# Working out the RMS norm's factor on a PSUM tile, with Newton's products in another order

## The chip, the core and the metric

The kernel runs on one core of a Trainium2 chip. The metric is the device time of one execution in microseconds (us). Before the change three executions took 826.66, 829.93 and 831.51 us: the median is 829.93 us.

## What is computed

Three blocks follow one another (cut from the reference):

```python
# 1 clustered attention, 2 batches x 8 heads, 768 tokens, head size 64
mask = q_assign[:, :, :, None] == k_assign[:, :, None, :]
scores = np.where(mask, scale * q @ k.T, -1e9); attn = softmax(scores); x = attn @ v
# 2 gated block on (1536, 512): RMS norm, two products to 1536, one back to 512
rms = np.sqrt(np.mean(x * x, axis=-1, keepdims=True) + 1e-06)
xn = x / rms * rms_g
g = xn @ w_gate
x = (g / (1 + np.exp(-g)) * (xn @ w_val)) @ w_out
# 3 second block: h = x @ w_in, s * relu(h)**2 + b, @ w_out2
```

The change lies in the line that computes `rms`: the kernel needs 1/rms for every token.

## The kernel before

**Stages.** Attention works head by head (16 heads, 8 of each batch). For each head the scores of 128 keys by 768 queries are made on PE (`scores`, L447 and L448), exponentiated on ACT (`expo`, L453), split into an fp16 high part (`cast`, on ACT at L460 or on POOL at L458) and an fp16 rest (`rest`, POOL, L464, tile `al`), and multiplied with the values on PE (`pv_chunk`, L487 and L477). Ahead of that, per head, PE makes row maxima of the scores (`rowmax`, L416, tile `mps`), which DVE reduces (`rowmax_out`, L424, tile `mt`). DVE also copies the head's result out (`pv_out`, L498 to L500, tile `xt`).

**The norm.** When a batch's 8 heads are done, `rms_sq` and `rms_sq2` (L516 to L524) square and sum them into `ss`, six columns for the six chunks of 128 tokens. `rms_scale` (from L528) adds the two halves of `ss` (L530), scales them (L531) and calls `rsqrt` (L504 on), which makes a first guess with integer operations on the bits (L506, L507) and refines it with three Newton steps of three instructions each (L509, L510, L511). That is 13 DVE instructions on tiles of 128x6 elements, and before the change every operand lies in SBUF. For each chunk, `rms_norm` (L539) then multiplies the row by the factor and by `g_row` into `xn`, PE transposes it (`rms_tr`, L546, tile `tr`), ACT makes the high part (`rms_x`, L553, `xh`) and DVE the low part (L555, `xl`).

**What follows.** The first gated-block products of batch 0 are mixed into the attention of batch 1 (`m_mm`, `m_pr`); the rest of both blocks comes after the attention, where PE works on long runs of matmuls (L623, L656, L658).

**What sets the order.** A planner (`Plan`) takes every step with an engine, a cost, its dependencies and a due time worked out from the table `P`, and writes one fixed instruction order for each engine. Buffers of a tag (`s` has 3 PSUM tiles, `g` has 2) are handed out in that order. Each engine then runs its own list in order and waits on semaphores. The pool of the tag `g` (`ps_g0`) takes over the PSUM of the second row-maximum tile when the plan's step `switch` runs.

The same `rsqrt` also serves `centroid_scale` at the very start of the kernel, on tiles of 128x1 that stay in SBUF.

Of the kernel before, what the change touches and what calls it, by code (L numbers as in the profile page):

```python
# [20 lines left out]
F32 = mybir.dt.float32  # L21
# [6 lines left out]
ALU = mybir.AluOpType  # L28
# [16 lines left out]
class Plan:  # L45
# [8 lines left out]
    def add(self, eng, dur, fn, r=(), w=(), new=(), prio=0.0, lat=None):  # L54
        deps = set()
        n = len(self.ops)
        for key in r:
            if key in self.last_w:
                deps.add(self.last_w[key])
        for key in w:  # L60
            deps.update(self.readers.get(key, ()))
            if key in self.last_w:
                deps.add(self.last_w[key])
        for key in r:
            self.readers.setdefault(key, []).append(n)
        for key in w:
            self.last_w[key] = n
            self.readers[key] = []
        for t in {key[:2] for key in (*r, *w)}:
            self.users.setdefault(t, []).append(n)  # L70
        self.ops.append((eng, dur, fn, deps, new, prio, lat))
# [74 lines left out]
def attention_moe_moe2_kernel(  # L146
# [18 lines left out]
    B, H, S, D = q.shape  # L165
# [5 lines left out]
    NCH = S // 128  # L171
# [8 lines left out]
    PSUM = bass.MemoryType.PSUM  # L180
    dma = nc.sync.dma_start
    act = nc.scalar.activation
    tt = nc.vector.tensor_tensor
    stt = nc.vector.scalar_tensor_tensor

    def pool(stack, name, bufs=1, **kw):
        return stack.enter_context(tc.tile_pool(name=name, bufs=bufs, **kw))
# [9 lines left out]
    ps_g = []  # L197
# [21 lines left out]
    sm = pool(att, "sm")  # L219
# [7 lines left out]
    ps_s = pool(att_a, "ps_s", P["b_s"], space=PSUM)  # L227
    ps_v = pool(att_a, "ps_v", P["b_pv"], space=PSUM)
    att_m = ExitStack()
# [8 lines left out]
    ss = [big.tile([128, NCH, 2], F32, name=f"ss{i}") for i in range(B)]  # L238
# [265 lines left out]
    def rsqrt(y, x, w):  # L504

        nc.vector.tensor_scalar(w.bitcast(I32), x.bitcast(I32), 1, None, op0=ALU.logical_shift_right)  # L506
        nc.vector.tensor_scalar(y.bitcast(I32), w.bitcast(I32), -1.0, float(0x5F3759DF), op0=ALU.mult, op1=ALU.add)  # L507
        for _ in range(3):
            tt(out=w, in0=y, in1=y, op=ALU.mult)  # L509
            stt(out=w, in0=w, scalar=-0.5, in1=x, op0=ALU.mult, op1=ALU.mult)  # L510
            stt(out=y, in0=w, scalar=1.5, in1=y, op0=ALU.add, op1=ALU.mult)  # L511

    def rms_sq(b, c, h0, h1, j):
# [12 lines left out]
    jk2 = {}  # L526

    def rms_scale(b):  # L528
        x, r, w = (sm.tile([128, NCH], F32, tag=f"{n}{b}", name=n) for n in ("rx", "rr", "rw"))
        tt(out=x, in0=ss[b][:, :, 0], in1=ss[b][:, :, 1], op=ALU.add)  # L530
        nc.vector.tensor_scalar(x, x, 1.0 / DM, 1e-6, op0=ALU.mult, op1=ALU.add)  # L531
        rsqrt(r, x, w)
        r_t[b] = r
        for t in range(b * S // TB, (b + 1) * S // TB):
            xh[t], xl[t] = new_x(t)
# [210 lines left out]
    add = pl.add  # L746
# [6 lines left out]
    def call(fn, *args):  # L753
        return lambda: fn(*args)
# [40 lines left out]
    def last_head():  # L795
        early.close()
        xpool[2] = xpool[3] = pool(ctx, "x1p", side="right")

    for i in range(NH):
        b, h = heads(i)  # L800
        p = i // 2

        def at(lead, more=0):
            return NCH * i - P[lead][b] - more + (P["ho"][i] if i < len(P["ho"]) else 0)

        if i % 2 == 0:
            if i:
                add("SP", 2.2, call(load, i), r=[("q4", 0, "m") if i == 2 else ("lseq", i - 2)], w=[("t", i), ("t", i + 1), ("lseq", i)], new=[("t", i), ("t", i + 1)],
                    prio=at("lq"), lat=5.2)
            add("SP", .48, call(load_v, i), r=[("q4", 0, "m")] if i == 2 else [], w=[("vr", i), ("vr", i + 1)], new=[("vr", i), ("vr", i + 1)],  # L810
                prio=at("lw"), lat=1.7)
            add("ACT", 1.03, call(v_square, i), r=[("vr", i), ("vr", i + 1)], w=[("v2", p)], new=[("v2", p)],
                prio=at("ly"))
# [26 lines left out]
        for c in range(NCH):  # L840
            add("PE", .36, call(rowmax, i, c), r=[("q4", i, x) for x in ("qh", "b1", "m")], w=[(mk(i, c), (i, c))], new=[(mk(i, c), (i, c))],
                prio=at("lm", -c))
            add("DVE", .95, call(rowmax_out, i, c), r=[(mk(i, c), (i, c)), *([("maxed", i, 0)] if c else [])], w=[("mt", i), ("maxed", i, c)], new=[("mt", i)] if c == 0 else (),
                prio=at("lm", -c))
# [4 lines left out]
        if P["nat"][i]:  # L849
            add("ACT", .19 + .05 * P["nat"][i], call(prep_v3, i), r=[("vr", i), ("vsc", p), ("vs", i, "h")], w=[("vs", i, "n"), ("loaded_v", i, "n")],  # L850
                prio=at("lv"))
        add("POOL", .08, call(prep_one, i), r=[("vs", i, "h"), ("vs", i, "n")], w=[("vs", i, "1")], prio=at("lv"))
        add("DVE", .2 * (NCH - P["nat"][i]), call(prep_v2, i), r=[("vr", i), ("vsc", p), ("vs", i, "h")], w=[("vs", i, "l"), ("loaded_v", i)], prio=at("lv"))
        for c in range(NCH):
            for e in range(2):
                add("PE", .36, call(scores, i, c, e), r=[("q4", i, x) for x in ("qh", "m", "x", "b1", "b2", "ql", "kl", "lt")],
                    w=[("s", (i, c, e)), ("scored", i, c, e)], new=[("s", (i, c, e))], prio=at("ls", -c))
                add("ACT", .49, call(expo, i, c, e), r=[("s", (i, c, e))], w=[("a", (i, c))],
                    new=[("a", (i, c))] if e == 0 else (), prio=at("ls", -c))
            if c >= NCH - P["nat"][i]:  # L860
# [3 lines left out]
                prio=at("lc", -c))  # L864
        for c0 in range(0, NCH, P["pvb"]):
# [5 lines left out]
                w=[("pv", i)], new=[("pv", i)] if c0 == 0 else (), prio=at("lp", -c0))  # L871
        add("DVE", 1.0, call(pv_out, i), r=[("pv", i), ("vsc", p)], w=[("xt", b, h)], new=[("xt", b)] if h == 0 else (),
            prio=at("lz"))
# [8 lines left out]
        if i == NH - 1:  # L882
            add("SP", 0.0, last_head, r=[(x, n) for x in ("loaded_u", "loaded_v") for n in range(NH)] + [("loaded_v", n, "n") for n in range(NH)] + [("scored", n, c, e) for n in range(NH) for c in range(NCH) for e in range(2)], w=[("r", 1)], prio=-1e5)
        if h == H - 1:
            add("DVE", 2.4, call(rms_scale, b), r=[("ss", b, c, x) for c in range(NCH) for x in (H - 3, H - 1)],
                w=[("r", b)], prio=at("lr"))
            for c in range(NCH):
                g = ("s", ("r", b, c))
                add("DVE", .89, call(rms_norm, b, c), r=[("r", b), ("g_row", 0), *(("xt", b, x) for x in range(H))],
                    w=[("xn", (b, c))], new=[("xn", (b, c))], prio=at("lr"))  # L890
                add("PE", .43, call(rms_tr, b, c), r=[("xn", (b, c))], w=[g], new=[g], prio=at("lr"))
                t = b * (S // TB) + c * 128 // TB
                add("ACT", .6, call(rms_x, b, c, 0), r=[g], w=[("x", t, "h", c)], prio=at("lr"))
                add("DVE", .68, call(rms_x, b, c, 1), r=[g, ("x", t, "h", c)], w=[("x", t, "l", c)], prio=at("lr"))
# [55 lines left out]
    def m_acc(n, t, c):  # L950
        project_add(pg_t.pop((n, t, "p", c)), t, c, TB, n == 0)

    def switch():
        att_m.close()
        ps_g.append(pool(att_m, "ps_g0", P["b_g"], space=PSUM))

    def m_xh(t, c):
        if c == 0:
            xh[t], xl[t] = new_x(t)
# [2 lines left out]
    def m_xl(t, c):  # L962
        nc.gpsimd.tensor_tensor(
            out=xl[t][:, c], in0=acc[t][:, c * TB:c * TB + TB], in1=xh[t][:, c].bitcast(F32), op=ALU.subtract
        )

    add("SP", 0.0, switch, r=[("maxed", H - 1, c) for c in range(NCH)], w=[("gsw", 0)], prio=-1e5)

    def gx(t, part):
        return [("x", t, part, c) for c in range(t * TB // 128, (t + 1) * TB // 128)]  # L970
# [80 lines left out]
```

## Time and profile before

| | us |
|---|---|
| median of three executions | 829.93 |
| lowest, highest | 826.66, 831.51 |
| the profiled execution, its own time | 827.66 |
| its span, first to last instruction | 825.7 |
| PE busy in the span | 780.9 |
| DVE busy | 519.4 |
| ACT busy | 469.1 |
| POOL busy | 444.4 |

The span is what the trace covers; 2.0 us lie around it. PE is TensorE's matmul, PEld its weight load, DVE VectorE, ACT ScalarE, POOL GpSimd, SP the queue that issues the DMAs. A duration in the trace runs from the start of an instruction to its end, so an instruction that is held up after its start shows a long duration and no idle time before it. In the table of stages, PEclk is the granted share of TensorE's full clock of 2.4 GHz; 0.50 is 1.2 GHz.

### The profile page before, as it was taken

How to read it: one execution, taken by the hardware profiler on the slowest of the kernel's cores; microseconds unless marked ns; L12 is line 12 of the kernel's file. 1: busy time of each engine (PE TensorE's matmuls, PEld its weight loads, DVE VectorE, ACT ScalarE, POOL GpSimd, SP SyncE). 2: the span in 40 equal slices, each digit the busy share in tenths (PEclk: the TensorE clock that was granted, in tenths of full speed). 3: DMA queues.
4: the chain of work that ended last, by engine and by line, in shares of the span. 5: the costliest groups of instructions: out<-in, count | busy, mean ns of one | idle time of the engine just before them, and what ended most of it. 6: DMA issues, size and time to landing. Idle time of an engine off the chain costs nothing.

```text
span 825.7 us, 14199 instructions
## 1 busy us (share of the span) xinstructions
PE 780.9 (95%) x5505; PEld 722.5 (88%) x5505; DVE 519.4 (63%) x845; ACT 469.1 (57%) x883; POOL 444.4 (54%) x400
## 2 busy tenths in 40 slices
PE   3899898699999799999999999999999999999998
PEld 1688776589998689999999999998999998989897
DVE  6789898898876676554645446554465555555533
ACT  5486778556858555442434435555566566665532
POOL 7599999677999534332323226455343343343421
PEclk9999999799999999999999999999999999999999
DMA  7498766155430223311311212220121121220012
GB/s 114 86 138 146 159 135 122 30 106 134 98 87 27 78 77 102 101 55 50 102 51 56 72 52 78 82 93 30 32 97 52 52 77 52 78 74 29 1 39 114
DMA packets 98818, 65.13 MB, mean 79 GB/s; under 512 B 64992, under 2 KB 89664, under 8 KB 98752
## 3 DMA queue, kind: packets, MB, share of 16 engines
q1 hardware_dynamic: 98752, 64.24, 31.3%
q8 instruction: 43, 0.70, 0.4%
q14 instruction: 23, 0.19, 0.1%
HBM read 48.45 MB, written 3.15 MB: 62 GB/s over the span
## 4 chain that ended last, share of the span: by engine, by line
PE 81%; DVE 10%; POOL 3%; issue 2%; DMA 2%; ACT 2%; SPq 0%; DVEq 0%; POOLq 0%
PE pg L623 28%; PE po L658 16%; PE po L656 10%; PE pl L623 10%; PE pv L487 4%; PE mps L416 4%; PE sps L447 3%; PE sps L448 3%; PE pv L477 2%; DVE mt L424 2%; PE pg L656 1%; DVE wa L610 1%; DVE vs L355 1%; DVE wa L611 1%; DMA q<-ot 1%
## 5 line engine op out<-in xcount | busy, mean ns | idle before, releaser
L646 POOL TENSOR_TENSOR gl<-hv,gh 128x384 fp32r<-128x384 f32 x104 | 107.2, 1030 | 214.0 <-ACT gh L645 195.2
L623 PE MATMUL pg<-xh,wh 128*128 128x384 f32 x480 | 162.1, 338 | 1.5 <-ACT wh L614 1.1
L623 PE MATMUL pg<-xh,wl 128*128 128x384 f32 x480 | 161.4, 336 | 0.7 <-POOL wl L617 0.7
L623 PE MATMUL pg<-xl,wh 128*128 128x384 f32 x480 | 161.2, 336 | 0.0
L617 POOL TENSOR_TENSOR wl<-wa,wh 128x512 fp32r<-128x512 f32 x74 | 95.9, 1296 | 115.8 <-ACT wh L614 110.1
L464 POOL TENSOR_TENSOR al<-a,ah 128x768 f16<-128x768 f32 x80 | 137.2, 1729 | 14.8 <-ACT ah L460 13.5
L610 DVE SCALAR_TENSOR_TENSOR wa<-wb,wa 128x512 int32<-128x512 f32 x74 | 54.2, 732 | 97.4 <-ACT wa L606 97.1
L666 DVE TENSOR_TENSOR acc<-po,acc 128x512 f32<-128x512 f32 (+1 forms) x160 | 95.1, 620 | 29.6 <-PE po L658 19.2
L453 ACT ACTIVATE a<-sps 128x384 f32<-128x384 f32 x192 | 86.7, 490 | 44.6 <-PE sps L448 42.8
L606 ACT ACTIVATE wa<-raw,ebias 128x512 f32<-128x512 int8 x74 | 56.2, 759 | 77.2 <-POOL wl L617 77.1
L424 DVE TENSOR_REDUCE mt<-mps 128x1 fp32r<-128x768 f32 x96 | 90.3, 944 | 13.9 <-PE mps L416 13.8
L623 PEld LDWEIGHTS pg<-xh,wh 128*128 128x128 f32 x480 | 90.1, 188 | 4.0 <-ACT wh L614 1.4
L623 PEld LDWEIGHTS pg<-xl,wh 128*128 128x128 f32 x480 | 90.1, 188 | 1.2
L623 PEld LDWEIGHTS pg<-xh,wl 128*128 128x128 f32 x480 | 90.0, 188 | 1.1 <-POOL wl L617 1.1
L643 DVE SCALAR_TENSOR_TENSOR th<-pg,th 128x384 f32<-128x384 f32 x64 | 35.5, 554 | 71.2 <-ACT th L642 71.0
L658 PE MATMUL po<-wh,gl 128*128 128x512 f32 x192 | 75.1, 391 | 0.6 <-POOL gl L646 0.6
L658 PE MATMUL po<-wl,gh 128*128 128x512 f32 x192 | 75.0, 391 | 0.0
L607 ACT ACTIVATE wb<-raw,ebias 128x512 f32<-128x512 int8 x74 | 56.6, 765 | 32.1 <-DVE wa L610 23.7
L658 PE MATMUL po<-wh,gh 128*128 128x512 f32 x192 | 74.7, 389 | 0.0
L447 PE MATMUL sps<-q 128*128 128x384 f32 x192 | 71.8, 374 | 2.9 <-ACT a L453 1.7
L614 ACT ACTIVATE wh<-wa 128x512 fp32r<-128x512 f32 x74 | 46.7, 631 | 48.3 <-PE pg L623 22.7
L611 DVE SCALAR_TENSOR_TENSOR wa<-raw,wa 128x512 int32<-128x512 int32 x74 | 72.4, 978 | 1.7
(134 smaller groups left out, 1746.5 us busy)
## 6 DMA issues: line engine op xcount, KB each, us to landing
raw<-in_moe_w_out_dram SPq DMA_DIRECT2D x30, 511.6 KB, 3.5
raw<-in_moe_w_in_dram SPq DMA_DIRECT2D x16, 510.5 KB
raw<-in_moe_w_gate_dram SPq DMA_DIRECT2D x14, 510.5 KB, 3.4
raw<-in_moe_w_val_dram SPq DMA_DIRECT2D x14, 510.5 KB, 3.4
q<-q SPq DMA_DIRECT2D x14, 384.0 KB, 4.6
q<-q SPq DMA_DIRECT2D x28, 192.0 KB, 4.1
vr<-in_v_dram SPq DMA_DIRECT2D x8, 384.0 KB
out_dram<-acc SPq DMA_DIRECT2D x12, 256.0 KB, 2.0
```

Of the source, the lines that this page charges most:

```text
L424: nc.vector.tensor_reduce(out=mt_of[i][:, c:c + 1], in_=m_t.pop((i, c))[:, :, 0:HALF], axis=AX.XY, op=ALU.max)
L447: nc.tensor.matmul(ps[:, 0:HALF], lhsT=x[:, 2, ks], rhs=x[:, 1, cs], start=True, stop=False)
L453: act(out=a_t[i, c][:, e * HALF:(e + 1) * HALF], in_=s_t.pop((i, c, e))[:, 0:HALF], func=ACTF.Exp, scale=scale)
L464: nc.gpsimd.tensor_tensor(out=al, in0=a_t.pop((i, c)), in1=ah_t[i, c], op=ALU.subtract)
L610: stt(out=ai, in0=b, scalar=2.0 ** 31, in1=a, op0=ALU.min, op1=ALU.subtract, reverse1=True)
L611: stt(out=ai, in0=low, scalar=5, in1=ai, op0=ALU.logical_shift_right, op1=ALU.bitwise_or)
L617: nc.gpsimd.tensor_tensor(out=l, in0=a, in1=h.bitcast(F32), op=ALU.subtract)
L623: nc.tensor.matmul(ps, lhsT=a[:, kk * 128:kk * 128 + 128], rhs=x[:, kk, :], start=(kk == m == 0), stop=(kk == KC - 1 and m == 2),)
L646: nc.gpsimd.tensor_tensor(out=gl, in0=hv, in1=gh.bitcast(F32), op=ALU.subtract)
L656: nc.tensor.matmul(ps, lhsT=a[:, cs], rhs=x, start=st[0], stop=st[1])
L658: nc.tensor.matmul(ps, lhsT=x[:, cs], rhs=a, start=st[0], stop=st[1])
L666: tt(out=ac, in0=ps, in1=ac, op=ALU.add)
```

## The change

The two scratch tiles of `rms_scale`, `x` and `w`, become columns 0 to 5 and 16 to 21 of one PSUM tile. Batch 0 takes that tile from the pool of the tag `g`, so `switch` now runs in the plan before batch 0's factor; batch 1 takes one of the three `s` tiles. The result `r` stays in SBUF. In each Newton step the first product is now x times y instead of y times y, and the second multiplies by y instead of x: the same value -0.5·x·y·y, worked out in another order.

```diff
--- before.py
+++ after.py
@@ -506,8 +506,8 @@
         nc.vector.tensor_scalar(w.bitcast(I32), x.bitcast(I32), 1, None, op0=ALU.logical_shift_right)
         nc.vector.tensor_scalar(y.bitcast(I32), w.bitcast(I32), -1.0, float(0x5F3759DF), op0=ALU.mult, op1=ALU.add)
         for _ in range(3):
-            tt(out=w, in0=y, in1=y, op=ALU.mult)
-            stt(out=w, in0=w, scalar=-0.5, in1=x, op0=ALU.mult, op1=ALU.mult)
+            tt(out=w, in0=x, in1=y, op=ALU.mult)
+            stt(out=w, in0=w, scalar=-0.5, in1=y, op0=ALU.mult, op1=ALU.mult)
             stt(out=y, in0=w, scalar=1.5, in1=y, op0=ALU.add, op1=ALU.mult)
 
     def rms_sq(b, c, h0, h1, j):
@@ -526,7 +526,9 @@
     jk2 = {}
 
     def rms_scale(b):
-        x, r, w = (sm.tile([128, NCH], F32, tag=f"{n}{b}", name=n) for n in ("rx", "rr", "rw"))
+        ps = ps_s.tile([128, 512], F32, tag="s", name="rps") if b else ps_g[-1].tile([128, 512], F32, tag="g", name="rpg")
+        x, w = ps[:, 0:NCH], ps[:, 16:16 + NCH]
+        r = sm.tile([128, NCH], F32, tag=f"rr{b}", name="rr")
         tt(out=x, in0=ss[b][:, :, 0], in1=ss[b][:, :, 1], op=ALU.add)
         nc.vector.tensor_scalar(x, x, 1.0 / DM, 1e-6, op0=ALU.mult, op1=ALU.add)
         rsqrt(r, x, w)
@@ -795,6 +797,10 @@
     def last_head():
         early.close()
         xpool[2] = xpool[3] = pool(ctx, "x1p", side="right")
+
+    def switch():
+        att_m.close()
+        ps_g.append(pool(att_m, "ps_g0", P["b_g"], space=PSUM))
 
     for i in range(NH):
         b, h = heads(i)
@@ -882,8 +888,11 @@
         if i == NH - 1:
             add("SP", 0.0, last_head, r=[(x, n) for x in ("loaded_u", "loaded_v") for n in range(NH)] + [("loaded_v", n, "n") for n in range(NH)] + [("scored", n, c, e) for n in range(NH) for c in range(NCH) for e in range(2)], w=[("r", 1)], prio=-1e5)
         if h == H - 1:
-            add("DVE", 2.4, call(rms_scale, b), r=[("ss", b, c, x) for c in range(NCH) for x in (H - 3, H - 1)],
-                w=[("r", b)], prio=at("lr"))
+            g = "s" if b else "g"
+            if b == 0:
+                add("SP", 0.0, switch, r=[("maxed", H - 1, c) for c in range(NCH)], w=[("gsw", 0)], prio=-1e5)
+            add("DVE", 2.4, call(rms_scale, b), r=[*([] if b else [("gsw", 0)]), *(("ss", b, c, x) for c in range(NCH) for x in (H - 3, H - 1))],
+                w=[("r", b), (g, ("n", b))], new=[(g, ("n", b))], prio=at("lr"))
             for c in range(NCH):
                 g = ("s", ("r", b, c))
                 add("DVE", .89, call(rms_norm, b, c), r=[("r", b), ("g_row", 0), *(("xt", b, x) for x in range(H))],
@@ -950,10 +959,6 @@
     def m_acc(n, t, c):
         project_add(pg_t.pop((n, t, "p", c)), t, c, TB, n == 0)
 
-    def switch():
-        att_m.close()
-        ps_g.append(pool(att_m, "ps_g0", P["b_g"], space=PSUM))
-
     def m_xh(t, c):
         if c == 0:
             xh[t], xl[t] = new_x(t)
@@ -963,8 +968,6 @@
         nc.gpsimd.tensor_tensor(
             out=xl[t][:, c], in0=acc[t][:, c * TB:c * TB + TB], in1=xh[t][:, c].bitcast(F32), op=ALU.subtract
         )
-
-    add("SP", 0.0, switch, r=[("maxed", H - 1, c) for c in range(NCH)], w=[("gsw", 0)], prio=-1e5)
 
     def gx(t, part):
         return [("x", t, part, c) for c in range(t * TB // 128, (t + 1) * TB // 128)]
```

No engine's order of instructions changes. The only engine whose list reads differently is DVE, at the two places where the factor is worked out and in the centroids' `rsqrt`. In this piece of DVE's list for batch 0, as it stood before, `rx` and `rw` are the two SBUF scratch tiles and `rr` is the result:

```order
L530 TENSOR_TENSOR rx<-ss_138 128x6
L531 TENSOR_SCALAR rx<-rx 128x6
L506 TENSOR_SCALAR rw<-rx 128x6
L507 TENSOR_SCALAR rr<-rw 128x6
L509 TENSOR_TENSOR rw<-rr 128x6
L510 SCALAR_TENSOR_TENSOR rw<-rw,rx 128x6
L511 SCALAR_TENSOR_TENSOR rr<-rw,rr 128x6
```

And the same piece now, where `rpg` is the PSUM tile (the next six rows repeat the last three in both):

```order
L532 TENSOR_TENSOR rpg<-ss_138 128x6
L533 TENSOR_SCALAR rpg<-rpg 128x6
L506 TENSOR_SCALAR rpg<-rpg 128x6
L507 TENSOR_SCALAR rr<-rpg 128x6
L509 TENSOR_TENSOR rpg<-rpg,rr 128x6
L510 SCALAR_TENSOR_TENSOR rpg<-rpg,rr 128x6
L511 SCALAR_TENSOR_TENSOR rr<-rpg,rr 128x6
```

The number and the place of the instructions are the same. Of the 13, only the first still reads nothing but SBUF (both halves of `ss`); the other twelve read at most one operand from SBUF, and each of them has one in PSUM.

## Rows read from the trace of the kernel before

**Rows 1.** The page, part 1: busy time, share of the span and instructions of each engine.

```profile
PE 780.9 (95%) x5505; PEld 722.5 (88%) x5505; DVE 519.4 (63%) x845; ACT 469.1 (57%) x883; POOL 444.4 (54%) x400
```

**Rows 2.** Stages of the span: stage, length, busy us (count) of PE, PEld, DVE, ACT, POOL; PEclk; DMA.

```profile
148.00:157.00 9.00, 2.81 (x15) 1.89 (x13) 8.59 (x15) 3.24 (x7) 6.78 (x8) 0.77 0.20 44
157.00:165.00 8.00, 8.00 (x70) 7.51 (x70) 5.59 (x8) 4.23 (x8) 3.47 (x2) 0.62 0.01 2
165.00:180.00 15.00, 13.60 (x168) 12.06 (x165) 14.37 (x18) 8.18 (x19) 9.52 (x6) 1.00 0.41 83
200.00:220.00 20.00, 20.00 (x194) 18.85 (x191) 15.34 (x26) 16.28 (x35) 17.36 (x12) 1.00 0.37 98
...
280.00:300.00 20.00, 17.09 (x101) 15.79 (x102) 18.25 (x38) 11.81 (x20) 6.89 (x6) 1.00 0.25 76
```

**Rows 3.** Who waited for whom, 147 to 165 us: total, times, longest.

```profile
POOL al L464 <- ACT ah L460: 6.9, 3, 6.1
...
PE mps L416 <- DVE mt L424: 5.9, 2, 5.7
```

**Rows 4.** VectorE in order, batch 0's factor: start us, us, engine, line.

```profile
147.83 0.49 DVE L530 TENSOR_TENSOR rx<-ss 128x6 f32<-128x6 f32 x1
148.36 0.74 DVE L531 TENSOR_SCALAR rx<-rx 128x6 f32<-128x6 f32 x1
149.14 1.57 DVE L506 TENSOR_SCALAR rw<-rx 128x6 int32<-128x6 int32 x1
...
152.35 0.72 DVE L509 TENSOR_TENSOR rw<-rr 128x6 f32<-128x6 f32 x1
...
153.31 1.49 DVE L511 SCALAR_TENSOR_TENSOR rr<-rw,rr 128x6 f32<-128x6 f32 x1
...
155.63 0.17 DVE L510 SCALAR_TENSOR_TENSOR rw<-rw,rx 128x6 f32<-128x6 f32 x1
155.83 0.17 DVE L511 SCALAR_TENSOR_TENSOR rr<-rw,rr 128x6 f32<-128x6 f32 x1
155.91 0.95 DVE L424 TENSOR_REDUCE mt<-mps 128x1 fp32r<-128x768 f32 x1
```

**Rows 5.** GpSimd in order, same stretch.

```profile
149.04 3.25 POOL L464 TENSOR_TENSOR al<-a,ah 128x768 f16<-128x768 f32 x2
152.23 0.83 POOL L458 CAST ah<-a 128x768 f16<-128x768 f32 x1
...
153.14 1.64 POOL L464 TENSOR_TENSOR al<-a,ah 128x768 f16<-128x768 f32 x1
160.86 1.65 POOL L464 TENSOR_TENSOR al<-a,ah 128x768 f16<-128x768 f32 x1 [6.09 <-ACT ah L460]
```

**Rows 6.** One line's instructions: count, duration ns min/median/max, first and last start.

```profile
L555 DVE TENSOR_TENSOR xl<-tr,xh x12: 674/679/692, 161.6 to 299.1; 128x512 fp32r<-128x512 f32 x12
...
L539 DVE SCALAR_TENSOR_TENSOR xn<-xt,rr,g_row x12: 732/743/2287, 156.8 to 294.8; 128x512 f32<-128x512 f32 x12
...
L424 DVE TENSOR_REDUCE mt<-mps x96: 910/947/959, 17.1 to 256.5; 128x1 fp32r<-128x768 f32 x96
...
L524 DVE TENSOR_REDUCE ss<-jk x2: 940/942/945, 145.5 to 279.3; 128x6 f32<-128x768 f32 x2
...
L498 DVE TENSOR_SCALAR dn<-pv,vsc x16: 183/224/227, 48.4 to 276.1; 128x6 f32<-128x6 f32 x16
```

**Rows 7.** GpSimd and VectorE in order, 168 to 171 us.

```profile
169.86 1.29 POOL L458 CAST ah<-a 128x768 f16<-128x768 f32 x1
...
168.19 2.29 DVE L539 SCALAR_TENSOR_TENSOR xn<-xt,rr,g_row 128x512 f32<-128x512 f32 x1
```

**Rows 8.** VectorE in order, batch 1's factor.

```profile
280.27 0.41 DVE L530 TENSOR_TENSOR rx<-ss 128x6 f32<-128x6 f32 x1
...
282.93 0.17 DVE L511 SCALAR_TENSOR_TENSOR rr<-rw,rr 128x6 f32<-128x6 f32 x1
283.01 0.69 DVE L610 SCALAR_TENSOR_TENSOR wa<-wb,wa 128x512 int32<-128x512 f32 x1
```

## The prediction

> **What bounds the kernel now.** Read four views in this order. The page's first part says that PE is busy for 95% of the span [rows 1], so a microsecond can be won only where PE stands still. The table of stages shows where that is: from 200 to 220 us PE works all 20.00 us, but from 148 to 157 only 2.81 of 9, while DVE works 8.59 of 9 [rows 2]. The list of waits names the wait: PE's row maximum L416 stands 5.7 us in one piece for DVE's L424, and POOL's `al` 6.1 us for ACT, which has no new scores [rows 3]. DVE's own list shows why L424 is late: before it stands the batch's factor, 13 instructions on 128x6 elements, and some of these tiny instructions take 0.49 to 1.57 us, while the same ones later take 0.17 [rows 4].
>
> POOL's list explains the long ones. L506 starts at 149.14 and ends at 150.71, when the first of POOL's two `al` ends (149.04 plus half of 3.25 is 150.67); L507, also 1.57 us, ends with the second at 152.3; L509 ends at 153.07 with POOL's cast (152.23 + 0.83); L511 ends at 154.80 with the next `al` (153.14 + 1.64 = 154.78) [rows 4, 5]. Each waits after its start for one POOL instruction to finish. From 154.8 on POOL stands still, and the remaining instructions take 0.17 us each, one every 0.20 [rows 4].
>
> **Whether a PSUM operand lifts that wait.** Compare lines with the same kind of neighbours on POOL. L539 reads two SBUF tensors and takes 732 to 2287 ns; L555 reads one from PSUM and one from SBUF, and its 12 instructions take 674 to 692 [rows 6]. The changed chain has that second form in all but its first instruction, which still adds two SBUF tiles. So I let that one keep its 0.49 us and free the other twelve.
>
> **The cost of each part, batch 0.**
> - *Waits taken away.* Over 0.17 us, L531 loses 0.57, L506 and L507 1.40 each, L509 0.55 and the first L511 1.32: together 5.24 us [rows 4]. The rest is unchanged, so L424 could start at 150.67 instead of 155.91.
> - *PSUM access.* No row shows DVE writing to PSUM. Reading costs nothing measurable: L424 reduces 768 elements from PSUM in 947 ns, L524 as many from SBUF in 942 [rows 6]. The other bound is L498, 128x6 from PSUM in 224 ns, against 171 at most for the SBUF form, though L498 also reads a scalar from a column [rows 4, 6]. That makes 0 to 0.05 us an instruction, 0 to 0.6 for twelve. I take the value near 0, since the reduce pair is the same operation at the same size. The first `xn` has to wait for POOL in any case (next point), which covers this term in batch 0.
> - *A new wait.* The twelve `xn` and `xl` behind the factor ran with little from POOL beside them. POOL stood still for 6.09 us until 160.86 [rows 5]. Now the first `xn` would start at about 151.5, inside POOL's `al` that ends at 152.29, so it runs to about 153.0 and the cast and the `al` behind it move by about 0.6, to an end at 155.4. That both sides push each other is visible at 168: `xn` takes 2.29 us there and POOL's next cast 1.29 instead of 0.83 [rows 5, 7]. The second `xn` is ready at about 153.9, waits for that `al`, runs until 156.1, and only then POOL begins the `al` that now begins at 160.86. So POOL gains 160.86 − 156.05 = 4.8 us. Both ends: if one more `xn` is held for a whole `al`, 5.24 − 1.65 = 3.6; at most, all of POOL's idle time, 6.1.
> - *TensorE's clock.* It averages 0.77 in 148 to 157 and 0.62 in 157 to 165 [rows 2], after the idle piece of 5.7 us. With an idle piece of about 0.5 us it may stay at the upper level. I credit nothing for that, since DVE and POOL set the pace here; it helps the upper end.
>
> I take 4.8. Behind it PE is 91% busy in 165 to 180 and without a gap in 200 to 220 [rows 2], with the same instruction order, so what arrives earlier stays earlier.
>
> **Batch 1.** Here POOL is quiet: the first addition takes 0.41 us, and every later one takes 0.17 [rows 8]. Nothing can be won, and DVE goes straight on to the weights (L610 at 283.01), in a stage where DVE works 18.25 of 20 us and PE has 2.9 us of gaps [rows 2, 8]. So the PSUM price of 0 to 0.6 us falls on the path; I put in 0.2. The `s` tile that the factor borrows holds nobody up, since the scores are over and the transposes need the factor anyhow. Batch 0's `g` tile and the earlier `switch` add no wait to any engine. The centroids' reordered products stay in SBUF and keep their count and sizes, so they cost nothing.
>
> **The Trainium skill on this.** The page "Perfetto Trace Analysis", section Optimizing Scalar/DVE Operations, speaks against the change: it gives DVE about 60 ns of fixed cost for SBUF and about 125 ns for PSUM. That is an estimate of 65 ns times 12, 0.8 us in each batch; batch 1 would then lose 0.8 and the sum would be −4.0 instead of −4.6. The pair 947 and 942 ns shows no such difference for reading; for writing no run here shows it.
>
> **The sum.** −4.8 + 0.2 = −4.6 us. The profiled execution took 827.66 us and its span 825.7; it lies 2.3 us under the median of 829.93. With the same difference the median becomes **825.3 us**. A measurement of this kernel can tell about 0.5%, 4.15 us, from no change; the forecast lies just outside that.
>
> **Rivals.**
> - *The gain is given back between 157 and 183.* DVE works 14.37 of 15 us in 165 to 180 [rows 2], and more of its two-SBUF instructions could now meet POOL. Two more waits of a whole `al` cost 2 x 1.65 = 3.3, leaving 1.3: 828.6 us. For it speaks the 2.29 us of `xn` at 168 [rows 7]; against it, that POOL and DVE both move by about the same amount.
> - *The clock falls all the same.* PE still does little from 149 to 152, and the lower level could come as it did before. PE was busy for all of 157 to 165 [rows 2], so that stretch would keep its length and only the earlier start, cut by the first `xn`'s wait of 0.8 and a half `al`, would be won: 5.24 − 0.8 − 0.8 = 3.6, or 826.5 with batch 1's 0.2.
> - *Slower: the wait is POOL's against DVE as such, not a matter of operands.* Its place is the same twelve instructions. All five waits stay, and the PSUM price is paid without return in both batches: 2 x 0.6 = 1.2, so 831.1 us. It decides against the change once the price exceeds the waits that are lifted. For it: L531 and L506 read a single SBUF tensor and waited too [rows 4], so two SBUF inputs are not the whole condition. Against it: the twelve steady L555, of which the first, at 161.6, ran inside POOL's `al` that starts at 160.86 [rows 5, 6].
>
> **How the numbers follow.** Forecast 0.60: its own spread from 3.4 to 6.1 us of gain puts 0.53 beyond 4.15 and 0.07 within. Given back 0.20: 0.17 within, 0.03 slower. Clock 0.10: within. Wait stays 0.10: 0.07 within, 0.03 slower by over 0.5%. That makes faster 0.53, same 0.41, slower 0.06. The range must take in the largest gain (829.93 − 6.1 = 823.8, and 2.4 less for half the spread of the three executions: 821.5 rounded) and the first two rivals; at the upper end I stop at 830.0, which leaves out the slower cases.
>
> **What would show it.** Right: the twelve instructions at 0.17 to 0.22 us in both batches, the first addition still stretched in batch 0, PE's longest wait for L424 near 0.5 us instead of 5.7, the next `al` after POOL's pause at about 156, the clock at 1.00 through 150 to 165. Wrong: any of the twelve at over 1 us beside an `al`; a first `xn` or later L355, L379, L611 longer than before by 1.6 us or more; or a chain in batch 1 that grows by more than 0.6 us.

## The result, and the profile after

| | before | after |
|---|---|---|
| median, us | 829.93 | 822.07 |
| lowest, highest, us (7 runs each) | 826.66, 832.42 | 818.40, 823.68 |
| ratio after to before, with its 95% interval | | 0.9898 [0.9875, 0.9922] |
| profiled execution, us | 827.66 | 818.40 |
| its span, us | 825.7 | 816.4 |

The kernel became 1.0% faster. The forecast was 825.3 us, a gain of 4.6. The two medians lie 7.9 us apart; the ratio on record, which is an estimate of its own and not the quotient of the two medians (0.9905), stands for about 8.5. The changed kernel was measured twice more, with ratios of 0.9896 [0.9860, 0.9931] and 0.9938 [0.9910, 0.9966]. Its 22 runs have a median of 823.46 us, the 76 runs of the kernel before in the same measurements and one other 829.98: 6.5 us apart. So two things need an explanation: what made 6.5 out of 4.6, and what scatters around it.

The page of after, part 1, to set beside [rows 1] (columns as there): PE's busy time falls by 3.6 us with as many matmuls, which a shorter wait alone would not do.

```profile
PE 777.3 (95%) x5505; PEld 717.4 (88%) x5505; DVE 515.9 (63%) x845; ACT 468.1 (57%) x883; POOL 445.4 (55%) x400
```

The stages of after, columns as in [rows 2]:

```profile
148.00:157.00 9.00, 7.34 (x91) 6.16 (x89) 9.00 (x10) 6.31 (x12) 8.49 (x7) 1.00 0.21 46
157.00:165.00 8.00, 6.96 (x45) 6.14 (x44) 7.58 (x10) 3.56 (x9) 6.69 (x4) 1.00 0.16 37
```

Before, PE did 2.81 us of work in 148 to 157, at a mean clock of 0.77, and then had 0.62. Now it does 7.34, and the clock is 1.00 in both stages. VectorE's list shows why (start us, us, engine, line):

```profile
144.87 0.50 DVE L532 TENSOR_TENSOR rpg<-ss 128x6 f32<-128x6 f32 x1
145.41 0.17 DVE L533 TENSOR_SCALAR rpg<-rpg 128x6 f32<-128x6 f32 x1
145.61 0.17 DVE L506 TENSOR_SCALAR rpg<-rpg 128x6 int32<-128x6 int32 x1
...
147.65 0.17 DVE L511 SCALAR_TENSOR_TENSOR rr<-rpg,rr 128x6 f32<-128x6 f32 x1
147.73 0.95 DVE L424 TENSOR_REDUCE mt<-mps 128x1 fp32r<-128x768 f32 x1
148.60 1.28 DVE L541 SCALAR_TENSOR_TENSOR xn<-xt,rr,g_row 128x512 f32<-128x512 f32 x1
149.80 0.94 DVE L424 TENSOR_REDUCE mt<-mps 128x1 fp32r<-128x768 f32 x1
150.67 2.18 DVE L541 SCALAR_TENSOR_TENSOR xn<-xt,rr,g_row 128x512 f32<-128x512 f32 x1
152.77 0.94 DVE L424 TENSOR_REDUCE mt<-mps 128x1 fp32r<-128x768 f32 x1
...
154.90 0.94 DVE L424 TENSOR_REDUCE mt<-mps 128x1 fp32r<-128x768 f32 x1
...
158.05 0.96 DVE L424 TENSOR_REDUCE mt<-mps 128x1 fp32r<-128x768 f32 x1 [0.35 <-PE mps L416]
```

The first addition, with its two SBUF operands, still takes 0.50 us; the other twelve take 0.16 or 0.17 each, one every 0.20. From the first addition to the L424 behind the chain it is 2.86 us, where it was 155.91 − 147.83 = 8.08 [rows 4]: 5.22 less. The new waits are there too: the first two `xn` take 1.28 and 2.18 us instead of 0.74. POOL and PE in the same stretch of after:

```profile
146.07 3.25 POOL L464 TENSOR_TENSOR al<-a,ah 128x768 f16<-128x768 f32 x2
149.28 1.28 POOL L458 CAST ah<-a 128x768 f16<-128x768 f32 x1
...
150.64 5.85 POOL L464 TENSOR_TENSOR al<-a,ah 128x768 f16<-128x768 f32 x3
157.14 1.65 POOL L464 TENSOR_TENSOR al<-a,ah 128x768 f16<-128x768 f32 x1 [0.65 <-ACT ah L460]
```

```profile
148.73 0.62 PE L416 MATMUL mps<-q 127*128 127x384 f32 x2 [0.46 <-DVE mt L424]
149.19 0.34 PE L447 MATMUL sps<-q 128*128 128x384 f32 x1
149.37 0.34 PE L448 MATMUL sps<-q 128*128 128x384 f32 x1
```

While the chain runs, POOL works without a pause (the two `al` from 146.07 to 149.3, casts before them), and of the chain only the first instruction notices it; behind the chain the two `xn` do. POOL's pause of 6.09 us [rows 5] is gone: three `al` follow one another, the second and third of 2.10 and 2.17 us, each beside an `xn`:

```profile
L464 POOL TENSOR_TENSOR al<-a,ah x3: 1660/2097/2174, 150.6 to 154.3; 128x768 f16<-128x768 f32 x3
```

PE waits 0.46 us for the L424 behind the chain, not 5.7 [rows 3], and two following score matmuls start 0.18 us apart. In batch 1 the chain reads, beside [rows 8]:

```profile
270.91 0.41 DVE L532 TENSOR_TENSOR rps<-ss 128x6 f32<-128x6 f32 x1
...
273.68 0.69 DVE L612 SCALAR_TENSOR_TENSOR wa<-wb,wa 128x512 int32<-128x512 f32 x1
```

That is 2.77 us from the addition to the weights, where it was 2.74.

### The profile page after: what moved, and what is told of

Same layout as the page of the kernel before. It is cut to its first block, busy times and chain, and to the rows that moved or that the text cites. A ratio compares the mean times of both kernels' runs of the same rounds, so it can differ in the third digit from the quotient of the medians.

```text
span 816.4 us, 14199 instructions
## 1 busy us (share of the span) xinstructions
PE 777.3 (95%) x5505; PEld 717.4 (88%) x5505; DVE 515.9 (63%) x845; ACT 468.1 (57%) x883; POOL 445.4 (55%) x400
## 4 chain that ended last, share of the span: by engine, by line
PE 82%; DVE 10%; POOL 3%; issue 2%; ACT 2%; DMA 1%; DVEq 0%; POOLq 0%
PE pg L625 28%; PE po L660 16%; PE po L658 10%; PE pl L625 10%; PE pv L487 4%; PE mps L416 4%; PE sps L447 3%; PE sps L448 3%; DVE mt L424 2%; PE pv L477 2%; PE pg L658 1%; DVE wa L612 1%; DVE xn L541 1%; DVE wa L613 1%; DVE w L379 1%
## 5 line engine op out<-in xcount | busy, mean ns | idle before, releaser
L424 DVE TENSOR_REDUCE mt<-mps 128x1 fp32r<-128x768 f32 x96 | 90.1, 942 | 11.0 <-PE mps L416 10.7
L447 PE MATMUL sps<-q 128*128 128x384 f32 x192 | 70.3, 366 | 2.8 <-ACT a L453 1.7
```

Source lines behind the costliest of these rows:

```text
L424: nc.vector.tensor_reduce(out=mt_of[i][:, c:c + 1], in_=m_t.pop((i, c))[:, :, 0:HALF], axis=AX.XY, op=ALU.max)
L447: nc.tensor.matmul(ps[:, 0:HALF], lhsT=x[:, 2, ks], rhs=x[:, 1, cs], start=True, stop=False)
```

## Where the difference of each profile lies

To compare profiles I cut each at three marks on VectorE: **A** is the first addition of batch 0's factor, **B** the L424 right behind the chain, and **C** the fourth L424 behind B (it starts at 167.31 us before, at 158.05 after). The column "start" says how much later than in the kernel before A comes, "rest" what the span gained or lost behind C. All in us.

| kernel | start | A to B | B to C | A to C against before | rest | span against before |
|---|---|---|---|---|---|---|
| before | 0 | 8.08 | 11.40 | 0 | 0 | 0 |
| changed, first | −3.0 | 2.86 | 10.32 | −6.3 | 0.0 | −9.3 |
| changed, second | +2.9 | 2.85 | 10.31 | −6.3 | 0.0 | −3.4 |
| changed, third | −2.5 | 2.86 | 10.31 | −6.3 | 0.0 | −8.8 |
| e1 products only | +2.5 | 8.10 | 10.89 | −0.5 | +4.5 | +6.5 |
| e2 `x` in SBUF | +3.2 | 5.57 | 10.22 | −3.7 | +3.8 | +3.3 |
| e3 batch 0 only | 0.0 | 2.87 | 10.31 | −6.3 | +4.3 | −2.0 |
| e4 batch 1 only | +1.6 | 8.09 | 11.03 | −0.4 | +1.7 | +2.9 |
| e5 PE filled, missed | +3.3 | 8.10 | 10.23 | −1.1 | +4.0 | +6.1 |
| e6 PE filled | +2.6 | 8.14 | 9.16 | −2.2 | −0.1 | +0.3 |
| e9 maxima in PSUM too | −1.0 | 2.82 | 11.08 | −5.6 | +3.7 | −2.9 |
| e10 PE kept busy | −1.1 | 2.87 | 10.31 | −6.3 | +1.5 | −5.9 |
| e12 PE kept busy, less | −4.1 | 2.87 | 10.31 | −6.3 | 0.0 | −10.4 |

In all profiles that hold the change in batch 0, with nothing else altered near it, the stretch gives the same 6.3 us. The columns "start" and "rest" move by several microseconds between executions of one kernel (−3.0 and +2.9 for the changed one) and make the scatter. So of the 9.3 us between the two profiles 6.3 lie where the change is. The stretch of the old chain varies as well: e1, e4 and e5, whose chain and whose 5.7 us of standing still are those of before, are 0.4 to 1.1 us shorter in it. Counted from these three the change gives 5.2 to 5.9 us there; e6 below shows what varies.

## The experiments

**e1 and e4: the new order of products alone; batch 1 alone.** e1 keeps both scratch tiles in SBUF:

```diff
-            tt(out=w, in0=y, in1=y, op=ALU.mult)
-            stt(out=w, in0=w, scalar=-0.5, in1=x, op0=ALU.mult, op1=ALU.mult)
+            tt(out=w, in0=x, in1=y, op=ALU.mult)
+            stt(out=w, in0=w, scalar=-0.5, in1=y, op0=ALU.mult, op1=ALU.mult)
```

> The kernel before with Newton's products in the new order alone; x and w stay in SBUF. Every instruction still reads and writes SBUF, in the same sizes. All theories expect no change: 829.9 us within 2, and a chain of batch 0 with the same long instructions beside POOL (about 5 us over 0.17 us each). A time near 822 would say that the gain has nothing to do with PSUM.

e4 has the whole change, the earlier `switch` too, but takes the PSUM tile for batch 1 only (the diffs of e3 and e4 are shown in part; the plan hands the tile over to match):

```diff
+        if b == 1:
+            ps = ps_s.tile([128, 512], F32, tag="s", name="rps")
+            x, w = ps[:, 0:NCH], ps[:, 16:16 + NCH]
+        else:
+            x, w = (sm.tile([128, NCH], F32, tag=f"{n}{b}", name=n) for n in ("rx", "rw"))
```

> The kernel before with only batch 1's factor on the PSUM tile, and Newton's new order. POOL is quiet there, and in the changed kernel the chain of batch 1 took the same 2.74 us from its first addition to the next instruction as before. Both theories expect no change: ratio 1.000 within 0.004. A gain of over 0.4% would say that batch 1 holds a part that batch 0 alone lacked.

Measured: e1 1.0004 [0.9977, 1.0031], e4 0.9984 [0.9959, 1.0009], both no difference that can be told from chance. e1's chain in batch 0 takes 8.10 us: the waits stay. e4's chain in batch 1 takes 2.78 us, so a PSUM operand costs these small instructions nothing that shows, and earns nothing where POOL is quiet.

**e3: batch 0 alone.**

```diff
+        if b == 0:
+            ps = ps_g[-1].tile([128, 512], F32, tag="g", name="rpg")
+            x, w = ps[:, 0:NCH], ps[:, 16:16 + NCH]
+        else:
+            x, w = (sm.tile([128, NCH], F32, tag=f"{n}{b}", name=n) for n in ("rx", "rw"))
```

> The changed kernel with batch 1's factor back in SBUF, Newton's new order kept. If the whole gain is batch 0's, the time is that of the changed kernel, 822 us within 1.5. If batch 1's PSUM operands cost 0 to 0.6 us as the prediction allowed, it is up to 0.6 faster; if batch 1 holds part of the gain, it is slower than 823.5.

Measured: 0.9928 [0.9896, 0.9959], a median of 825.02 us, which by the expectation would say that batch 1 holds part of the gain. The medians can't decide that: the unaltered changed kernel itself had 825.25 in one of its measurements, and e4 shows no gain of batch 1. The stretch is that of the whole change, 13.18 us from A to C. Its profile shows only −2.0 us, since it lost 4.3 behind C. The stage of e3 in which that happened, columns as in [rows 2]:

```profile
268.60:282.20 13.60, 12.16 (x41) 11.15 (x40) 8.53 (x24) 6.02 (x9) 2.21 (x3) 0.50 0.14 41
```

TensorE is at its lower level of 1.2 GHz there. In the profiles of before and after the mean of the granted clock in 260 to 290 is 1.00. The kernels e1, e2, e5 and e9 show such pieces between 267 and 291 us as well, e4 a shorter one: six of the thirteen profiles, each of which lost 1.7 to 4.5 us behind C. They come with the change and without it.

**e2: only the scratch `w` in PSUM.** `x` stays in SBUF, the products keep their old order. It asks what decides about the wait: the operands read, or the place written. The diff is against the kernel before and shown in part.

```diff
-        x, r, w = (sm.tile([128, NCH], F32, tag=f"{n}{b}", name=n) for n in ("rx", "rr", "rw"))
+        ps = ps_s.tile([128, 512], F32, tag="s", name="rps") if b else ps_g[-1].tile([128, 512], F32, tag="g", name="rpg")
+        w = ps[:, 16:16 + NCH]
+        x, r = (sm.tile([128, NCH], F32, tag=f"{n}{b}", name=n) for n in ("rx", "rr"))
```

> The changed kernel with only w in the PSUM tile and Newton's products in the old order; x is in SBUF. By the theory that what counts is the operands read from SBUF, the scaling of x (SBUF to SBUF) and, where POOL works, the product y times y (two reads of SBUF) still wait, while the other Newton instructions, which read w from PSUM and one SBUF tile, do not; the first guess's shift reads x from SBUF and writes PSUM, and is open. So 1 to 3 waits of up to 1.57 us stay in batch 0 and the time lies between the two kernels, 823 to 828 us. If any PSUM operand frees an instruction, only the scaling waits and the time is 822 to 824.

VectorE and POOL of e2, in order (start us, us):

```profile
151.53 0.74 DVE L533 TENSOR_SCALAR rx<-rx 128x6 f32<-128x6 f32 x1
152.31 0.17 DVE L506 TENSOR_SCALAR rpg<-rx 128x6 int32<-128x6 int32 x1
152.51 0.17 DVE L507 TENSOR_SCALAR rr<-rpg 128x6 int32<-128x6 int32 x1
152.71 1.18 DVE L509 TENSOR_TENSOR rpg<-rr 128x6 f32<-128x6 f32 x1
...
154.33 1.16 DVE L509 TENSOR_TENSOR rpg<-rr 128x6 f32<-128x6 f32 x1
```

```profile
152.21 3.25 POOL L464 TENSOR_TENSOR al<-a,ah 128x768 f16<-128x768 f32 x2
```

Both `al` run from 152.21 to 155.4. Beside them the scaling L533, SBUF to SBUF, waits to the end of the cast before them (152.25); L506, SBUF to PSUM, and L507, PSUM to SBUF, don't wait; L509, which reads `y` twice from SBUF, waits 1 us beside each `al` although it writes to PSUM. So it is no matter of VectorE against POOL as such, and both halves of the change are needed: `x` in PSUM for the scaling, and the new order so that no product reads two SBUF operands. The Trainium skill, "SBUF — State Buffer", section Who interferes with whom, has this rule: two SBUF inputs, or a copy, cast or tensor_scalar in a mode that takes both ports, share a port pair with GpSimd, which one of the two holds as an exclusive lock; with at most one SBUF input and no such mode nothing is shared. The rows agree (1.18 and 1.16 us against 0.17); the mode itself no row here shows.

The time of e2 is 0.9991 [0.9967, 1.0015], a median of 828.91 us, a miss: 823 to 828 were expected. Its stretch is 3.7 us shorter than that of the kernel before, and 2.5 to 3.3 shorter than those of e1, e4 and e5; the interval of its runs reaches down to a gain of 2.7 us. The mean granted clock of its runs is 0.990, as that of the kernel before: its profile still has a low piece behind the chain (157.0 to 160.4 us), and it lost 3.2 us before A, where the clock was low from 126.3 to 133.1, and 3.8 in low pieces behind C. What of that is chance I can't tell.

**e5 and e6: PE filled during the wait, the chain untouched.** The question is what the clock is worth in 157 to 165. Both kernels are the one before, with 28 added matmuls whose result nobody reads, in the hope of keeping TensorE at its upper level:

```diff
+        if (i, c) == (H + 2, 2):
+            pd = ps_g[-1].tile([128, 512], F32, tag="g", name="busy")
+            for _ in range(28):
+                nc.tensor.matmul(pd[:, 0:HALF], lhsT=x[0:127, 1, 0:128], rhs=x[0:127, 2, 0:HALF], start=True, stop=True)
```

e5 had them at `(i, c) == (H, 2)`.

> The kernel before with 28 more matmuls of 128x384 on PE, into an unused PSUM tile, in the piece where PE waits 5.7 us for DVE; DVE's chain and its waits are untouched. They take about 28 x 0.175 = 4.9 us of that piece. Theory A: the low clock level after the idle piece cost about 3 us that the change gave back; then the granted clock stays at 1.00 and the time falls by 2 to 3.5 us, to 826.5 to 828. Theory B: POOL's and DVE's instructions set the pace there and the clock cost nothing; then the clock stays at 1.00 and the time is 829.9 within 1.

Measured: 1.0032 [1.0009, 1.0055], a miss. The matmuls ran from 118.2 to 123.3 us, two heads before the wait, and PE still stood 5.7 us. So it does not test what it was built for. e6 has them in the right place:

> The same question as the run with 28 more matmuls before, with the matmuls now in front of the row maximum on which PE stands 5.7 us (third chunk of the eleventh head); there they sat two heads earlier, at 118 us, where they cost 3.4 us. DVE's chain and its waits are untouched. Theory A: the low clock level behind the idle piece cost about 2.9 us (matmuls every 0.32 instead of 0.175 us from 156.9 to 163.1); then the clock stays at 1.00 there, DVE's row maximum that stood at 167.3 comes 1 to 3 us earlier after the end of the chain, and the median falls by 1 to 3 us. Theory B: POOL and DVE set the pace; the clock stays at 1.00 and the distance from the end of the chain to that row maximum stays at 11.4 us.

Measured: 0.9964 [0.9935, 0.9993]. TensorE of e6 in order, where L420, L451 and L428 are the L416, L447 and L424 of the others, and two of its stages:

```profile
153.67 5.04 PE L418 MATMUL busy<-q 127*128 127x384 f32 x28
159.56 0.62 PE L420 MATMUL mps<-q 127*128 127x384 f32 x2 [0.85 <-DVE mt L428]
160.02 0.34 PE L451 MATMUL sps<-q 128*128 128x384 f32 x1
160.20 0.34 PE L452 MATMUL sps<-q 128*128 128x384 f32 x1
```

```profile
151.00:160.00 9.00, 7.66 (x41) 6.74 (x40) 8.62 (x14) 3.24 (x7) 6.41 (x7) 1.00 0.21 46
160.00:168.00 8.00, 7.83 (x99) 6.98 (x98) 7.56 (x11) 5.51 (x10) 4.91 (x3) 1.00 0.00 0
```

And three stages and two matmuls of the kernel before:

```profile
152.90:156.90 4.00, 0.00 (x0) 0.00 (x0) 3.73 (x11) 0.00 (x0) 1.88 (x4) 0.50 0.03 8
156.90:163.10 6.20, 6.18 (x50) 5.78 (x51) 4.56 (x6) 3.43 (x6) 2.01 (x2) 0.50 0.01 3
163.10:168.00 4.90, 4.90 (x56) 4.79 (x54) 3.60 (x5) 2.45 (x5) 2.99 (x2) 1.00 0.00 0
```

```profile
157.73 0.52 PE L447 MATMUL sps<-q 128*128 128x384 f32 x1
158.05 0.52 PE L448 MATMUL sps<-q 128*128 128x384 f32 x1
```

In the kernel before TensorE stood still to 156.9, was at half its clock from 152.9 and worked at that level until 163.1: score matmuls start 0.32 us apart. In e6 the clock holds, they start 0.18 apart, and from B to C it is 9.16 us instead of 11.40, while the chain keeps its 8.14. So in this pair of profiles the lower clock cost 2.24 us behind the wait, without any part of the change; the forecast of theory A was 1 to 3.

What it costs depends on where the low piece lies. Five profiles have the same chain of 8.1 us, and all but e6 the same 5.7 us in which PE stands still:

| kernel | low clock behind B, us | B to C, us |
|---|---|---|
| e6 | 0 | 9.16 |
| e5 | 4.1 | 10.23 |
| e1 | 6.0 | 10.89 |
| e4 | 6.4 | 11.03 |
| before | 7.2 | 11.40 |

From B to C it takes the longer, the more of the low clock lies behind B, by some 0.3 us for each microsecond of it. The profile of the kernel before lost most; the other three lost 1.1 to 1.9 us. VectorE of e6 at B, at the third L424 behind it and at C:

```profile
158.56 0.95 DVE L428 TENSOR_REDUCE mt<-mps 128x1 fp32r<-128x768 f32 x1
159.43 0.74 DVE L543 SCALAR_TENSOR_TENSOR xn<-xt,rr,g_row 128x512 f32<-128x512 f32 x1
...
164.58 0.95 DVE L428 TENSOR_REDUCE mt<-mps 128x1 fp32r<-128x768 f32 x1
...
167.72 0.96 DVE L428 TENSOR_REDUCE mt<-mps 128x1 fp32r<-128x768 f32 x1 [0.34 <-PE mps L420]
```

**e9: the maxima in PSUM as well.** The same idea carried one place further: the changed kernel, with the row maxima `mx` of the cluster assignment in spare columns of the PSUM tile `asps`, so that L379's comparison reads one SBUF operand (one of three places of the edit):

```diff
-        mx = sm2.tile([128, n, 1], F32, tag="mx", name="mx")
+        mx = mx_t.pop(i)
```

> The changed kernel with one more tile moved: the 12 maxima per head of the cluster choice go into spare columns of the PSUM tile that the scores came from, so that the comparison reads one SBUF and one PSUM tensor. Its 16 instructions took 357 to 1436 ns, 801 on average. By the operand theory all 16 fall to about 360 to 420 ns, some 6 to 7 us of DVE time in all; on the path perhaps 2 to 4 us of that, so 817 to 821 us. Against it: the PSUM tile is held about 1.5 us longer, 16 times, and PE may wait for it with its scores; then the time is 822 or more.

Measured: 0.9909 [0.9874, 0.9944], 824.70 us, a miss: no better than the changed kernel beside it (e8: 0.9896, 823.95 us), though the intervals leave room for a gain of a microsecond or two. The comparison in e9 (first row) and in the kernel before (second), durations in ns min/median/max:

```profile
L380 DVE TENSOR_TENSOR w<-as,asps x16: 353/354/355, 10.4 to 195.3; 128x192 bf16<-128x192 f32 x16
```

```profile
L379 DVE TENSOR_TENSOR w<-as,mx x16: 357/718/1436, 10.4 to 202.0; 128x192 bf16<-128x192 f32 x16
```

Every wait of that line is gone, some 7 us of VectorE's time against the kernel before and 8 to 10 against the three profiles of the changed one, and the kernel ends no earlier. VectorE waits more for PE's row maxima instead: 7.1 us between 20 and 145 us, before 3.9. What the expectation feared, PE's wait for the tile, is not it: TensorE stands 5.2 us ahead of the products for `asps` in that piece, before 5.5. So much of what VectorE gained went into waiting for PE; that a freed microsecond counts only where PE waits for VectorE is what these rows suggest, and no run tests it further.

**e8 and e11: the changed kernel again**, in two other measurements. Their edit is the change itself.

> The changed kernel once more, on the same chip as the others. The trace of the stretch from 144 to 175 us gives 6.4 us; what the first measurement showed beyond that (8.5) should be chance in where the clock falls elsewhere. So 0.992 (0.989 to 0.995) and a local gain of 6.4 us within 0.3 again. If the ratio is 0.990 or lower again, the change also gains outside that stretch.

> The changed kernel a third time, beside the one with more matmuls on the same chip. 0.990 (0.986 to 0.993) if the first two measurements stand; a local gain of 6.4 us between 144 and 175 us.

Measured: 0.9896 [0.9860, 0.9931] and 0.9938 [0.9910, 0.9966]. The two fall on either side of what was expected: by e8's expectation its 0.9896 would say that the change also gains elsewhere, and e11's 0.9938 lies above its range of 0.986 to 0.993. The three profiles agree to 0.02 us from A to C and lose or gain nothing behind it; they differ by up to 5.9 us ahead of A. Of the 22 runs, the 8 whose recorded clock is 1.000 average 820.8 us, the 14 others 824.5; but those 8 run from 818.40 to 824.27 themselves.

So the clock is not all of the scatter. In the profile of the first measurement the score matmuls are 0.18 us apart from 29 us on, in that of e8 only from 34.4, and from 34 us to the end the granted clock is 1.00 in both. At 42 us e8 is 1.5 us behind, at 70 us 5.5, and at A 5.9. Between 48 and 68 us its L379 and L355, which read two SBUF tensors each, took 3.4 us longer. The three L379 there, first measurement and then e8 (ns, min/median/max):

```profile
L379 DVE TENSOR_TENSOR w<-as,mx x3: 566/593/845, 48.8 to 62.9; 128x192 bf16<-128x192 f32 x3
```

```profile
L379 DVE TENSOR_TENSOR w<-as,mx x3: 1128/1366/1906, 50.4 to 67.1; 128x192 bf16<-128x192 f32 x3
```

That is the kind of wait that the change takes from the factor, and it fell differently in two executions of one kernel. Why it did no run tests.

**e10 and e12: PE kept busy at the start and near the end.** If pieces of low clock elsewhere make much of the scatter, then filling PE's waits there should take it away. Both kernels are the changed one with added matmuls whose result nobody reads: e10 has 14 between 9 and 25 us, and 3 ahead of each of the last head's three products that wait for POOL; e12 has 7 and 1 ahead of each (the trace shows each of them as two matmuls). The helper, and one of its places in e12:

```diff
+    def busy(n, p, tag):
+        if not bz or bz[-1][0] != tag:
+            bz.append((tag, p.tile([128, 512], F32, tag=tag, name="busy")))
+        for _ in range(n):
+            nc.tensor.matmul(bz[-1][1][:, 0:32 * H], lhsT=ident, rhs=cqk.rearrange("p h c -> p (h c)"), start=True, stop=True)
...
+                if i == NH - 1 and c >= 2 and m == 2 and qc == 0:
+                    busy(1, ps_s, "s")
```

> The changed kernel with 23 more matmuls of 128x256 into an unused PSUM tile, where PE waits anyway: 14 between 9 and 25 us, and 9 before the last head's three products that wait for POOL (about 267 us). Nothing else changes. In the traces so far the clock rises only at 28 to 34 us, and in 6 of the 9 profiles it falls again for 3 to 14 us between 267 and 291, which cost about 4 us. If idle pieces of PE are what lets it fall, the clock now rises before 25 us and stays at 1.00 to the end, and the time falls by 2 to 5 us against the changed kernel, to 819 to 822. If the matmuls only lie in the way, or the clock does not follow them, it is the changed kernel's time or up to 4 us more.

> The changed kernel with 10 instead of 23 more matmuls at the same places (7 between 9 and 25 us, one before each of the last head's three products that wait for POOL), so that they fit into PE's idle pieces: with 23 the first row maximum came 2.0 us later and the three products together 1.6 us later. If the clock still rises before 25 us and does not fall at 260 to 290, the time is that of the run with 23 less 1.5 to 3 us: 819 to 821. If 10 are too few, it rises at 28 to 34 again and the time is the changed kernel's, 822 to 825.

Measured: e10 0.9908 [0.9883, 0.9933], 821.95 us; e12 0.9866 [0.9826, 0.9905], 818.27 us, six runs from 817.37 to 821.14. In e10 the filling stood in the way: the first row maximum starts at 18.07 us, in the changed kernel at 16.04, and 1.5 us are lost behind C. By 38 us all but 0.3 of the 2.0 is made up, but at A it is 1.9 us behind again, and 1.1 of that arises between 74 and 84 us, at a clock of 1.00. Its clock rises at 14.7 us and is low once more from 89.8 to 93.2. In e12 the first row maximum starts at 16.08, and nothing is lost behind C; its time is a little below the 819 to 821 expected. What is to be won at the start is seen where the first scores are made, two in a row in the kernel before and then two in e12 (L462 and L463 there):

```profile
29.45 0.52 PE L447 MATMUL sps<-q 128*128 128x384 f32 x1
29.77 0.52 PE L448 MATMUL sps<-q 128*128 128x384 f32 x1
```

```profile
28.14 0.34 PE L463 MATMUL sps<-q 128*128 128x384 f32 x1
28.31 0.34 PE L462 MATMUL sps<-q 128*128 128x384 f32 x1
```

The stages of e12, columns as in [rows 2]:

```profile
10.00:20.00 10.00, 7.45 (x28) 4.45 (x26) 8.55 (x15) 7.45 (x13) 6.91 (x8) 0.82 0.95 122
20.00:30.00 10.00, 8.78 (x40) 6.14 (x39) 9.53 (x17) 3.07 (x7) 2.35 (x2) 0.84 0.50 108
260.00:290.00 30.00, 25.26 (x194) 22.17 (x190) 22.08 (x45) 16.54 (x28) 12.36 (x10) 1.00 0.23 70
```

TensorE of e12 reaches its upper level at 13.0 us, falls once more from 16.4 to 23.3, and keeps it from there to the end, through the stage in which six of the profiles fell; the matmuls of the kernel before are 0.32 us apart until 33.4. A comes 4.1 us earlier in e12. It is the fastest of all kernels run: its runs lie within 3.8 us, those of the changed kernel within 8.7 (818.40 to 827.07, median 823.46). It was timed against the kernel before and not side by side with the changed one, so its lead of some 5 us over the latter rests on medians of different measurements; its profile ends 1.1 us before the earliest of the changed kernel's, all of it won ahead of A.

## Why the prediction was right and wrong

- **The waits: right, to 0.02 us.** Five instructions waited on POOL, and a PSUM operand in place of an SBUF one lifts it: 5.24 us forecast, 5.22 measured. e1 shows that the order of products alone does nothing, e2 which operands decide. The first addition keeps its wait, as said.
- **The PSUM price: right to take it near nothing.** Twelve instructions at 0.17 us one every 0.20, batch 1's chain 2.77 instead of 2.74 us; I had put in 0.2. The 0.8 us that were estimated from the Trainium skill's "Perfetto Trace Analysis", section Optimizing Scalar/DVE Operations, are not there, for reading or for writing: batch 1's chain grew by 0.03.
- **The new waits: right in kind, wrong in what they leave.** The two `xn` take 1.28 and 2.18 us, where the forecast comes to 1.5 and 2.2. But I made POOL's next `al` wait for the end of the second `xn`; it starts at about 152.3, beside it, and takes 2.10 us instead of 1.65. Counted from A to its start, that is 7.4 us where it was 13.03 [rows 4, 5], a gain of 5.6 and not 4.8; to its end, a gain of 5.2. What the two long `xn` cost is seen against e6, whose first two `xn` meet no `al`: from B to the third L424 behind it, 154.90 − 147.73 = 7.17 us in after and 164.58 − 158.56 = 6.02 in e6, so 1.15. The forecast had let only 0.4 of the 5.24 us go to these waits.
- **The clock: here the forecast failed.** The step read "I credit nothing for that, since DVE and POOL set the pace here". PE at its lower clock set it too. The trace of the kernel before said so: behind the chain VectorE's L424 waits for PE, twice before 161 us.

```profile
157.97 0.96 DVE L424 TENSOR_REDUCE mt<-mps 128x1 fp32r<-128x768 f32 x1 [0.44 <-PE mps L416]
...
160.74 0.96 DVE L424 TENSOR_REDUCE mt<-mps 128x1 fp32r<-128x768 f32 x1 [1.16 <-PE mps L416]
```

  The term is worth 2.24 us by e6, counted from the profile of the kernel before, and 1.1 to 1.9 counted from e1, e4 and e5. The sum of the stretch is then −5.22 − 2.24 + 1.16 = −6.3, where the last term is what remains when e6's 9.16 from B to C becomes 10.32; the 1.15 of the two `xn` are nearly all of it. The medians of the 22 and 76 runs are 6.5 us apart. Without the clock the same sum gives −4.1: that the forecast of 4.8 came as near as it did is luck in part, since it took the new waits 0.7 us too small as well. The prediction's opening has the same slip, that a microsecond can be won only where PE stands still: PE was busy for all of 157 to 165, at 0.62 of its clock [rows 2].
- **The rest of the first measurement's 8.5 us** can't be put down to the change. In the profiles it lies ahead of A, where no instruction was altered but the centroids' products, and there three executions of the changed kernel differ by 5.9 us. No low piece lies there in the profiles of before and after: the clock rises at 33.4 us in one and at about 28 in the other, which goes with 1.5 us at 44 us, and another 1.5 us arises up to A at a clock of 1.00, from a cause that stays open.
- **The rivals.** "The gain is given back between 157 and 183" fell: behind C the distance stays. "The clock falls all the same" fell in all three profiles of the changed kernel. "Slower: POOL against DVE as such" fell with e2. The lower end of the range comes out of its own sum as 821.4, not 821.5, which changes nothing here.

**Open** is why the clock falls at 267 to 291 us, and at 90 to 134, in some executions and not in others, and whether the change makes that rarer. The mean clock of the runs is 0.998 for the first measurement of the changed kernel, 0.990 for the one before, and the piece at 152.9 to 163.1, 10.2 us at half the clock, explains 5.1 / 826 = 0.006 of that difference. e6, which fills only that wait, has 0.995 where the kernel before has 0.989 in the same measurement; so most of the difference needs no other pieces. Open is also what made e12 fastest, beyond its earlier start.

## What to carry to other kernels

A VectorE instruction that is long beside a GpSimd instruction and short elsewhere is waiting, though no idle time shows it: count its SBUF operands, and move one to a spare PSUM tile; for 128x6 elements that cost nothing here. When a change removes a long wait of TensorE, look at the granted clock and the spacing of matmuls behind that wait: 5.7 us of standing still cost 1.1 to 2.2 us more afterwards, by how much of the low clock lay behind it. And see which engine waits for which behind the place before you let a second gain go for nothing.

## What the runs showed of the hardware beyond that

- A 128x6 instruction that reads one SBUF tensor and writes SBUF waits for POOL (0.74 us in e2, up to 1.57 in [rows 4]); one that reads SBUF and writes PSUM doesn't. L506 is both: 1.57 us in the kernel before, 0.17 in e2, each time beside an `al`.
- A kernel with ten added matmuls that compute nothing of use is the fastest here: 0.9866 [0.9826, 0.9905] against 0.9896 to 0.9938 without them, in other measurements and with intervals that partly overlap. Twenty-three gave 0.9908.
- Executions of one program differ by the clock's low pieces (one of 13.6 us, from 268.6, goes with 4.3 us lost in e3) and, at the same clock, by how VectorE's two-SBUF instructions fall beside POOL (3.4 us between two executions of the changed kernel); its 22 runs spread over 8.7 us.
- The column of the granted clock shows 1.00 before its first change: in the kernel before it does so for 20 to 30 us, where score matmuls are 0.32 us apart, as they are at 0.50 in 156.9 to 163.1. At the start the spacing has to be read.
